# Attention and token/channel mixer on one core: the first seven slots laid out by hand, token weights loaded plainly, a last output tile sent in pieces

## The chip, the cores and the metric

The kernel runs on one core of one Trainium2 chip. A core has a matrix engine (TensorE, "PE" in the profile, its weight loads "PEld"), a vector engine (VectorE, "DVE"), an activation engine (ScalarE, "ACT"), a general engine (GpSimd, "POOL") and a queue engine (SyncE, "SP") that here only issues DMA transfers. Each runs its own list of instructions in order and waits on semaphores. The metric is the time of one execution on the device in microseconds (us), the median of several runs.

## What is computed

The reference is cosine attention followed by a mixer (batch 8, 12 heads, sequence 448, head size 64):

```python
q_n = q / (norm(q) + 1e-06);  k_n = k / (norm(k) + 1e-06)
scores = q_n @ k_n.T / tau
attn = exp(scores - max);  attn = attn / (sum(attn) + 1e-09)
x = attn @ v                                   # (8, 448, 768) once the heads are side by side
h = relu(x.T @ w_tok1) @ w_tok2                # over the sequence: 448 -> 256 -> 448
u = x + h.T
h2 = relu(u @ w_ch1) @ w_ch2                   # over the channels: 768 -> 1536 -> 768
out = u + h2
```

Since the scores are bounded, the kernel takes the exponential without subtracting the maximum.

## The kernel before, in words

Two heads make a pair, six pairs a batch, 48 pairs in all. Three pairs are a half (the index `n` of the loads), which is loaded, normed and cast together. The 448 rows of a sequence are three blocks of 128 and 64 extra rows; names with an x (`squares_x`, `scaled_x`, `score_x`) treat the extra rows.

For a pair p the steps are these. `squares` (L174 on ACT, L176 on POOL or VectorE) and `sums` (L189, L193 for the extra rows, both VectorE) give sums of squares. `rnorms` (L197 to L200) turns them into 1/(norm + 1e-6) by four activations: logarithm, exponential of half of it, logarithm of that plus 1e-6, exponential of the negative. `scaled` (L207) and `scaled_x` (L213, L218) multiply K and Q by it into the fp16 tile `kq`. `tpose` (L239, L243, L244, TensorE) transposes it into PSUM, `qk_copy` (L257, VectorE) takes it out. `score` (L297) and `score_x` (L304) multiply, and ACT takes the exponential (L298, L305). `pv` (L318, L320) multiplies with V and, on VectorE, divides by the row sum (L323, L324). `m_tok1` (L338, L341) and `m_tok2` (L357, L362, L364) are the token mixer. When a batch has its six pairs, its channel units `m_ch1` (L385, ACT L387) and `m_ch2` (L399, VectorE L402, stores L407 to L410) go into a queue, and `feed` takes units from it between the steps of later pairs. `busy` issues matmuls whose result nobody uses.

The order of the work on each engine is the order of the program text, since the schedule is manual. After a prologue for pair 0 the loop runs over slots i: a slot does the scores of pair i, `pv` of pair i−1, the token mixer of pair i−2, and norms, scaling and transposes ahead for later pairs. Tables (`sq_at`, `sum_at`, `rn_at`, `sc_at`, `cast_at`, `tok_at`, `tok2_at`) say in which slot such a step stands. `FIRST` is 6: from slot 6 on there are channel units to feed. `JOIN` is 12; up to pair 14 the transposes are TensorE's, and after that they are DMA transposes.

Loads of Q, K and V are issued on SP in order, at the start of a slot; each waits until its buffer is free. The weights are loaded on POOL's queue and cast from fp32 to fp16 in flight: `weights_tok` (L141 to L144) after the prologue, `weights_ch1` (L154) in slots 2 and 5, `weights_ch2` (L158) in slots 7 and 8. `place_w2` (L147, L150, VectorE) rearranges the second token weight at the end of slot 2. PSUM has four general buffers (tag "b", two kilobytes per partition each) that all the products share in turn, and two of double size for the scores.

The last batch's units run when nothing else is left: twelve of `m_ch1`, then `m_ch2` for the row blocks 0, 1, 2 and the block of extra rows, in two halves of 384 columns each. The block of extra rows carries 64 rows of each of two batches and is stored by two transfers (L409, L410).

## Time and profile before

| what | us |
|---|---|
| time, median of 5 runs | 401.42 (401.3 to 402.39) |
| the profiled execution, its own time | 403.68 |
| its span, first to last instruction | 401.5 |
| TensorE busy | 386.0 |
| ScalarE busy | 225.6 |
| GpSimd busy | 209.0 |
| VectorE busy | 204.8 |

The span is the stretch that the trace shows; the time of an execution is measured around it. Busy time of TensorE counts the fillers, and its matmuls overlap, so that a full TensorE is not one at its peak. In the table of stretches, the columns after the time are the busy us of each engine with the number of instructions, the granted clock of TensorE (1 is full), the share of DMA time and GB/s. A line of the timeline is start, duration, engine, line, operation, output and input tiles, and in brackets the idle time before it and who ended that. A line of the waits is the waiting engine, tile and line, then who was waited for, with the total in us, the number of times and the longest.

### The profile page before, as it was taken

How to read it: one execution, taken by the hardware profiler on the slowest of the kernel's cores; microseconds unless marked ns; L12 is line 12 of the kernel's file. 1: busy time of each engine (PE TensorE's matmuls, PEld its weight loads, DVE VectorE, ACT ScalarE, POOL GpSimd, SP SyncE). 2: the span in 40 equal slices, each digit the busy share in tenths (PEclk: the TensorE clock that was granted, in tenths of full speed). 3: DMA queues.
4: the chain of work that ended last, by engine and by line, in shares of the span. 5: the costliest groups of instructions: out<-in, count | busy, mean ns of one | idle time of the engine just before them, and what ended most of it. 6: DMA issues, size and time to landing. Idle time of an engine off the chain costs nothing.

```text
span 401.5 us, 9113 instructions
## 1 busy us (share of the span) xinstructions
PE 386.0 (96%) x3646; PEld 227.1 (57%) x3646; DVE 204.8 (51%) x463; ACT 225.6 (56%) x407; POOL 209.0 (52%) x306
## 2 busy tenths in 40 slices
PE   8789999998999999999999999999999999999995
PEld 3356465565556565566555565566555665565562
DVE  5788789465453665355544654455534353242021
ACT  5998699633666447655657436755667326601400
POOL 4987495598292949485673919486764400000000
PEclk9899999999999999999999999999999999999999
DMA  8999999999887599999996699869842733022012
GB/s 220 278 245 246 240 171 214 224 269 236 168 168 182 120 245 186 196 188 218 233 169 167 113 256 210 200 153 227 180 112 51 157 85 66 16 67 91 2 78 78
DMA packets 137194, 67.51 MB, mean 168 GB/s; under 512 B 93184, under 2 KB 133568, under 8 KB 137152
## 3 DMA queue, kind: packets, MB, share of 16 engines
q1 hardware_dynamic: 132976, 61.36, 70.4%
q0 software_dynamic: 3632, 5.18, 7.2%
q8 instruction: 28, 0.46, 0.5%
q10 hardware_dynamic: 544, 0.39, 0.3%
q14 instruction: 14, 0.11, 0.1%
HBM read 43.38 MB, written 11.01 MB: 135 GB/s over the span
## 4 chain that ended last, share of the span: by engine, by line
PE 39%; POOL 29%; issue 17%; DMA 6%; ACT 4%; DVE 3%; SPq 1%; ACTq 0%; POOLq 0%; DVEq 0%
PE psF L399 14%; PE psG L385 12%; POOL kq L207 10%; POOL sq L176 9%; DMA xv<-in_v_dram 5%; PE psO L318 3%; POOL kq L218 3%; POOL sqx L176 3%; PE psS L297 3%; ACT pt L298 2%; PE psR L338 2%; PE psU L357 2%; POOL vt L164 2%; POOL vx L168 1%; DMA km<-in_k_dram 1%
## 5 line engine op out<-in xcount | busy, mean ns | idle before, releaser
L298 ACT ACTIVATE pt<-psS 128x896 f16<-128x896 f32 x141 | 122.2, 916 | 64.6 <-PE psS L297 64.5
L385 PE MATMUL psG<-ut,wc1t 128*128 128x448 f16 x576 | 120.7, 353 | 0.0
L399 PE MATMUL psF<-wc2t,gt 128*128 128x384 f16 x672 | 116.3, 326 | 1.9 <-DVE ost L402 1.9
L387 ACT ACTIVATE gt<-psG 128x448 f16<-128x448 f32 x96 | 52.5, 547 | 74.5 <-PE psG L385 74.3
L207 POOL TENSOR_TENSOR kq<-km,rn 128x384 f16<-128x384 f32 x47 | 39.6, 843 | 94.8 <-ACT rn L200 93.5
L399 PEld LDWEIGHTS <-gt 128*128 128x128 f16 x672 | 64.2, 98 | 43.2 <-issue 3.3
L385 PEld LDWEIGHTS <-wc1t 128*128 128x128 f16 x576 | 53.2, 98 | 46.5 <-issue 4.4
L402 DVE TENSOR_TENSOR ost<-psF,ur 128x384 f32<-128x384 f32 x56 | 31.1, 556 | 76.3 <-PE psF L399 76.3
L318 PEld LDWEIGHTS <-pt 128*128 128x128 f16 x1152 | 52.7, 98 | 15.0 <-issue 3.4
L318 PE MATMUL psO<-vt,pt 128*128 128x65 f16 x1152 | 57.5, 194 | 0.0
L189 DVE TENSOR_REDUCE ssq<-sq 128x12 f32<-128x768 f32 (+1 forms) x49 | 45.2, 931 | 21.0 <-POOL sq L176 17.2
L297 PE MATMUL psS<-qk 64*128 64x448 f16 x282 | 41.1, 358 | 2.4 <-ACT pt L298 2.3
L324 DVE TENSOR_TENSOR x<-psO,rec 128x256 f16<-128x256 f32 x96 | 40.7, 424 | 3.3
L320 PE MATMUL psO<-vx,pt 128*128 128x130 f16 x192 | 41.8, 218 | 0.0
L323 DVE RECIPROCAL rec<-psO 128x4 f32<-128x4 f32 x96 | 17.1, 178 | 47.6 <-PE psO L320 47.4
L207 POOL TENSOR_TENSOR kq<-qm,rn 128x384 f16<-128x384 f32 x47 | 39.0, 829 | 0.0
L176 POOL TENSOR_TENSOR sq<-km 128x384 f32<-128x384 f32 x42 | 34.5, 823 | 2.7 <-DMA km<-in_k_dram 2.5
L338 PE MATMUL psR<-x,w1t 128*128 128x128 f16 x384 | 29.4, 219 | 0.1
L367 DVE TENSOR_TENSOR ut<-psU,xT 128x448 f16<-128x448 f32 (+2 forms) x39 | 17.6, 476 | 20.1 <-PE psU L357 20.0
L357 PE MATMUL psU<-w2t,r 128*128 128x448 f16 x96 | 25.9, 353 | 0.7 <-DVE x L324 0.4
L305 ACT ACTIVATE pt<-psX 128x448 f16<-128x448 f32 x48 | 26.5, 553 | 0.0
L176 POOL TENSOR_TENSOR sq<-qm 128x384 f32<-128x384 f32 x30 | 24.7, 823 | 0.8
(75 smaller groups left out, 324.5 us busy)
## 6 DMA issues: line engine op xcount, KB each, us to landing
vm<-in_v_dram SPq DMA_DIRECT2D x16, 576.0 KB, 5.6
out_dram<-ost SPq DMA_DIRECT2D x24, 384.0 KB, 3.8
qm<-in_q_dram SPq DMA_DIRECT2D x15, 576.0 KB, 5.2
km<-in_k_dram SPq DMA_DIRECT2D x15, 576.0 KB, 5.1
wc1t<-in_moe_w_ch_dram POOLq DMA_DIRECT2D x2, 1152.0 KB, 13.9
wc2t<-in_moe_w_ch_dram POOLq DMA_DIRECT2D x2, 1152.0 KB, 14.7
out_dram<-ost SPq DMA_DIRECT2D x8, 192.0 KB, 4.0
xq<-in_q_dram SPq DMA_DIRECT2D x7, 192.0 KB, 5.7
```

The lines of the kernel that those rows point to most:

```text
L176: eng.tensor_tensor(out=out, in0=src, in1=src, op=ALU.mult)
L189: nc.vector.tensor_reduce(out=ssqs[p // HP % 3][:, lo + 6 * a0:lo + 6 * a1], in_=sq[p][:, a0:a1].rearrange("p a g e -> p (a g) e"), axis=A ...
L207: eng.tensor_tensor(out=kqs[n % 2][:, j, a, 0:NC, :].rearrange("p c (g e) -> p g c e", g=2), in0=src, in1=_bcast_free(rn, E), op=ALU.mult)
L297: nc.tensor.matmul(psS[:, g, 0:S], qk[r, P * c:P * (c + 1)], qk[r, 512:512 + S], start=True, stop=True)
L298: nc.scalar.activation(out=pt[:, 2 * S * c:2 * S * (c + 1)].rearrange("p (g s) -> p g s", g=2), in_=psS[:, :, 0:S], func=AF.Exp, scale=inv ...
L318: nc.tensor.matmul(psO[:, mm, E1 * g:E1 * (g + 1)], pt[:, at:at + P], vt[:, 2 * j + g, c, 0:E1], start=(g == 0 and c == 0), stop=False)
L320: nc.tensor.matmul(psO[:, mm, :], pt[:, PX + lo:PX + lo + P], vx[:, j, 0:2 * E1], start=False, stop=True)
L324: nc.vector.tensor_tensor(out=xs[p][:, 2 * a:2 * a + 2, :].rearrange("p m (g e) -> p m g e", g=2), in0=o[:, :, :, 0:E], in1=_bcast_free(re ...
L338: nc.tensor.matmul(psR[:, tt, :], w1t[:, m, tt * P:(tt + 1) * P], xs[p][:, m, :], start=(m == 0), stop=(m == NC))
L385: nc.tensor.matmul(psG[:], wc1t[:, dt, ct * P:(ct + 1) * P], ut[:, dt, sp], start=(dt == 0), stop=(dt == DT - 1))
L387: nc.scalar.activation(out=gt[:, ct, sp], in_=psG[:], func=AF.Relu)
L399: nc.tensor.matmul(psF[:], gt[:, ct, lo:lo + P], wc2t[:, ct, dh * DH:(dh + 1) * DH], start=(ct == 0), stop=(ct == CT - 1))
```

## The change

It rewrites the prologue and slots 1 to 6, and the end.

- The token weights are loaded as fp32 by three plain transfers on SP, behind the first loads and ahead of those of slot 0. `place_w1` (new, slot 2) and `place_w2` (now slot 3) cast them on VectorE.
- `rnorms` is split: `norms` does the first two activations, and `inverses` adds 1e-6 and takes the reciprocal on VectorE. The prologue's pairs 1 and 2 and the extra rows, and half 1, use the two; other places keep the four activations.
- In the prologue the norms, scaling and transposes of pair 0 stand ahead of the sums of pair 1. Q of pair 0 gets a PSUM tile of its own. There are 14 fillers at the start instead of 18, and fillers are added between later steps. VectorE takes part of the scaling of pair 1 and all extra rows of half 0. The squares of pair 3 stand in the prologue.
- Slots 1 and 2 are written out. All squares of half 1 come by slot 1, all its scaling by slot 2. The extra rows of half 1 are scaled in two steps.
- Slots 3 to 6 take the token mixer in a changed order; in slot 6 ACT does the relu of pair 5 and the evictions of the second token product of pairs 4 and 5.
- The last batch computes its block of extra rows second. Its last row block is computed in pieces of 384, 256 and 128 columns, each stored on its own.

The core of the diff:

```diff
     def weights_tok():
-        nc.gpsimd.dma_start(out=w1t[:, 0:NC, :], in_=moe_w_tok1[0:SM].rearrange("(p c) t -> p c t", c=NC))
-        nc.gpsimd.dma_start(out=w1t[0:XR, NC, :], in_=moe_w_tok1[SM:S])
-        w2n.append(mix.tile([P, TT, S], FP16, name="w2n", tag="gt16", bufs=1))
-        nc.gpsimd.dma_start(out=w2n[0][:], in_=moe_w_tok2.rearrange("(tt p) s -> p tt s", p=P))
+        t = mix.tile([P, NC * T + T + TT * S], FP32, name="wtok", tag="gt16", bufs=1)
...
+        nc.sync.dma_start(out=wtok[0], in_=moe_w_tok1[0:SM].rearrange("(p c) t -> p c t", c=NC))
+        nc.sync.dma_start(out=wtok[1], in_=moe_w_tok1[SM:S])
+        nc.sync.dma_start(out=wtok[2], in_=moe_w_tok2.rearrange("(tt p) s -> p tt s", p=P))
+
+    def place_w1():
+        nc.vector.tensor_copy(out=w1t[:, 0:NC, :], in_=wtok[0])
+        nc.vector.tensor_copy(out=w1t[0:XR, NC, :], in_=wtok[1])
...
-    def rnorms(n, c0=0, c1=45):
+    def norms(n, c0=0, c1=45):
         ssq, rn = ssqs[n % 3][:, c0:c1], rns[n % 3][:, c0:c1]
         nc.scalar.activation(out=rn, in_=ssq, func=AF.Ln, bias=tiny[:])
         nc.scalar.activation(out=rn, in_=rn, func=AF.Exp, scale=0.5)
+
+    def inverses(n, c0=0, c1=45):
+        rn = rns[n % 3][:, c0:c1]
+        nc.vector.tensor_scalar_add(out=rn, in0=rn, scalar1=EPS_NORM)
+        nc.vector.reciprocal(out=rn, in_=rn)
...
-        busy(w, 18)
+        busy(w, 14)
         squares(0, nc.scalar, nc.scalar)
         sums(0, 0, 1)
         sums(0, 1, 2)
+        rnorms(0, 9, 21)
         squares(1, nc.scalar, nc.gpsimd)
-        rnorms(0, 9, 21)
+        squares_x(0, nc.scalar, nc.gpsimd)
+        scaled(0, nc.vector, nc.vector)
+        tpose_main(0, pst, 0)
+        nc.scalar.copy(out=qks[0][:, 0:SM], in_=pst[:, 0:SM])
+        tpose_main(0, psq, 1)
+        nc.vector.tensor_copy(out=qks[0][:, 512:512 + SM], in_=psq[:, 512:512 + SM])
         sums(1)
...
         sums_x(0)
...
         score_main0(0, 2)
+        norms(0, 0, 33)
+        inverses(0, 0, 33)
+        score_main0(1)
         squares(2, nc.scalar, nc.gpsimd)
...
         scaled_x(0, nc.vector, 0, 1)
...
+        scaled(1, nc.gpsimd, nc.vector)
+        scaled_x(0, nc.vector, 1, HP)
         score_rest0()
         score_x(0)
-        weights_tok()
+        busy(w, 3)
+        norm_begin(3, nc.scalar, nc.gpsimd)
+        sums(2)
+        qk_copy(1, tpose(1))
+        norms(0, 33, 45)
+        inverses(0, 33, 45)
         cast_v(0)
-        scaled(2, nc.gpsimd)
+        scaled(2, nc.gpsimd, nc.gpsimd)
...
+            elif i == 1:
+                score(1, 0, 2)
+                score(1, 1)
+                squares(4, nc.scalar, nc.gpsimd)
+                pv(0, 0)
+                sums(3)
+                score(1, 2)
+                score_x(1)
+                next_qk(2)
+                squares(5, nc.scalar, nc.gpsimd)
+                sums_x(1)
+                norms(1, 0, 21)
+                sums(4)
+                inverses(1, 0, 21)
+                sums(5)
+                scaled(3, nc.gpsimd, nc.gpsimd)
+                scaled_x(1, nc.gpsimd, 0, 1)
+                pv(0, 1)
+            elif i == 2:
+                score(2, 0, 2)
+                score(2, 1)
+                norms(1, 21, 45)
+                pv(1, 0)
+                inverses(1, 21, 45)
+                idle(4)
+                score(2, 2)
+                score_x(2)
+                next_qk(3)
+                place_w1()
+                pv(1, 1)
+                idle(2)
+                scaled(4, nc.gpsimd, nc.gpsimd)
+                scaled_x(1, nc.gpsimd, 1, HP)
+                cast_v(1)
+                scaled(5, nc.gpsimd, nc.gpsimd)
+                weights_ch1(0)
             elif 0 < i < NP_ALL and not (i > JOIN and i % 2):
-                score(i, 0, 2 if i < 4 else 0)
+                score(i, 0)
                 score(i, 1)
+                if i == 3:
+                    m_tok1(0)
+                    place_w2()
+                if i == 4:
+                    tok2(1)
+                if i < FIRST:
+                    m_tok1(i - 2)
...
             if i == FIRST:
-                next_sq([9])
-                m_tok1(i - 2)
                 pv(i - 1, 0)
+                m_tok1(i - 2)
                 pv(i - 1, 1)
-                tok2(i - 2)
-                m_tok1(i - 1)
+                scaled_x(2, nc.vector, 0, 1)
+                norm_sums(7)
+                m_tok2(i - 2, nc.scalar)
+                m_tok1(i - 1, nc.scalar)
                 next_qk(i)
-                tok2(i - 1)
+                tok2(i - 1, nc.scalar)
+                next_sq([9])
                 norm_sums(8)
...
+        last = b == B - 1
+        for m in (0, NC, 1, 2) if last else range(NC + b % 2):
+            for i0, i1 in ((0, 3), (3, 5), (5, 6)) if last and m == 2 else ((0, 3), (3, 6)):
+                units.append((ns(P * (i1 - i0), CT), lambda m=m, i0=i0, i1=i1:
+                              m_ch2(b, m, i0, i1, last and m == 2)))
```

`idle(n)` takes a PSUM tile and runs n fillers into it. In `m_ch2` the arguments i0 and i1 are the first and last block of 128 columns, and the last argument sends the piece as soon as it is evicted.

## The prediction

> **What bounds the kernel now.** I read the busy table by stretches first, because the shares of the page are means over stages with different limits.
>
> ```profile
> 10.00:14.00 4.00, 1.43 (x15) 0.67 (x16) 3.27 (x8) 3.55 (x9) 3.92 (x7) 1.00 1.14 306
> 14.00:18.00 4.00, 4.00 (x35) 1.85 (x31) 2.66 (x5) 3.94 (x12) 3.80 (x7) 0.57 1.16 246
> 18.00:22.00 4.00, 3.02 (x41) 1.73 (x40) 3.44 (x8) 3.90 (x10) 3.50 (x5) 1.00 1.18 271
> 22.00:26.00 4.00, 3.54 (x48) 2.16 (x45) 3.02 (x9) 3.61 (x9) 3.09 (x5) 1.00 1.17 245
> 30.00:34.00 4.00, 3.63 (x57) 2.54 (x55) 3.96 (x9) 3.10 (x7) 2.00 (x4) 1.00 1.09 256
> ```
>
> The columns are PE, weight loads, DVE, ACT, POOL, clock, DMA share, GB/s. From 10 to 34 us four engines are nearly full at once and TensorE waits for them; from 14 to 18 its clock is 0.57. After 60 us TensorE hardly idles: in the table of waits of that stretch it waits for anything but itself only 3.2 us, of which these two count:
>
> ```profile
> PE psF L399 <- DVE ost L402: 1.9, 2, 1.1
> POOL vt L164 <- DMA vm<-in_v_dram: 4.8, 1, 4.8
> ```
>
> They are one story: POOL's cast of the fifth V half waits for its load until 76.4, its squares end at 81.5, VectorE's sums at 82.5, and TensorE idles 0.83 before 83.1 and 1.05 before 91.6. What arrives early at 80 us can wait there. Then the end of the timeline and the head's anchors:
>
> ```profile
> 27.16 0.90 POOL L154 DMA_DIRECT2D wc1t<-in_moe_w_ch_dram  x1
> ...
> 42.40 1.30 PE L385 MATMUL psG<-ut,wc1t 128*128 128x448 f16 x6
> ...
> 396.60 0.56 DVE L402 TENSOR_TENSOR ost<-psF,ur 128x384 f32<-128x384 f32 x1 [1.39 <-PE psF L399]
> 397.19 0.50 SPq L409 DMA_DIRECT2D out_dram<-ost  x1
> 397.74 0.58 SPq L410 DMA_DIRECT2D out_dram<-ost  x1
> ```
>
> The first channel weights are issued at 27.16, land 13.9 us later by the rows of that line (41.1), and are first used at 42.40: 1.3 us of slack. The last matmul ends at 396.58, and 4.9 us of span follow.
>
> **What the skill says.** "SBUF — State Buffer", Who interferes with whom: GpSimd and a VectorE copy, cast or two-input operation share a port pair as a lock, and the later one blocks. The trace agrees: VectorE's 64x128 product at 10.69, beside POOL products, took 0.89, while a 128x384 one beside an idle POOL took 0.55. "DMA: Bandwidth & Descriptors", Queues, rings and completion order: an engine takes turns between queues packet by packet. It agrees: from 36 to 37 us POOL's queue moved 99 packets and SP's 102. "TensorE: Matmul & The Clock Gate", What's actually happening: a cold array runs at half rate and is warm after some 3.4 us of work. The halving agrees (filler matmuls 0.43 us apart until 7.3, then about half that); the warming took 5.9 us here.
>
> **The change part by part.** Durations are distances between neighbours in the timeline.
>
> *First scores.* VectorE now does sums(1) at 6.83 ahead of the scaling of pair 0 (7.71), whose norms are ready at 6.91. After: scaling at 6.93, 0.78 earlier. Fourteen fillers end at 7.35, so TensorE is free for the transposes; with its own PSUM tile the Q copy need not follow ACT's copy. Scores start near 9.15 instead of 10.08: −0.9.
>
> *The rest of pair 0.* sums(1) 0.87 and sums_x 0.66 now follow the Q copy (8.6): 10.2. norms 0.6: 10.8. The inverses on VectorE are two operations on 33 columns; the nearest row is the 4-column reciprocal, 0.18, so 0.3 together (bounds 0.2 and 0.5): 11.1. The extra-row scaling for pair 0, partly blocked by POOL's scaled(1), 1.3 (it took 1.8 before): 12.4. The transposes that wait for it started at 12.56, so the 0.9 is spent. sums(2) no longer stands before the copies (13.1 instead of 13.4), but VectorE has new work before qk_copy(1): half of scaled(1) 0.5, the extra rows of pairs 1 and 2 0.8 (bounds 0.7 and 1.5), sums(2) 0.9: copy from 15.3 to 15.9 instead of 15.45 to 16.1. Score(1) then starts near 15.95, not 16.32, on a warm array: −0.4.
>
> *Slots 1 and 2.* VectorE then has inverses 0.3, cast 0.73, pv 0.55, sums(3) 0.87, copy(2) 0.57, sums_x 0.66, sums(4) 0.87, inverses 0.3: 4.8, with 0.5 of waiting for pv's matmuls, so the inverses for pair 3 are ready at 21.3. POOL gets scaled(3) then; before, it began at 19.77. It loses the three token-weight issues (2.4 us, 12.84 to 15.2), half of scaled(1) 0.8 and 1.5 of extra rows, but 4.7 us saved are idled away, first for the K load of pairs 3 to 5 (some 13.7, from bytes queued ahead of it at the shown rates), then for those inverses. scaled(3) 1.6, its extra rows 1.1: 24.0 against 23.74. Score(3) starts near 25.4, before 25.6: −0.2.
>
> *Slot 3.* VectorE: place_w1 (768 and 256 columns from fp32; from the 1152-column cast, 0.73) 0.7, pv 0.55, cast 0.73, relu 0.34, place_w2 1.15 (as before, though it reads fp32), relu 0.34, pv 0.55, copy(4) 0.57: 4.9 from 25.1, so score(4) near 30.1, before 30.24. VectorE is the bound there.
>
> *Slots 4 to 6.* tok2(1) moves into slot 4 (0.6 more), tok2 copies and the relu of pair 5 move to ACT, which idled 4.3 us before 43.7; cover is plain. TensorE's own rows (score 0.49, tok1 0.45, tok2 0.57, pv 0.5 twice, score and extra rows 0.5, transposes 0.62) carry it to the first channel unit near 41.7: −0.7.
>
> *What is late next.* POOL's issue of the channel weights now stands behind scaled(5): from 21.3, scaled(3) 1.6, rows 1.1, scaled(4) 1.6, rows 1.5, casts 0.8, scaled(5) 1.6 = 29.5, 2.3 later. The landing is 12.3 (the shortest such row, a wc2t) to 13.9 later: 41.8 to 43.4. TensorE, there at 41.7, waits up to 1.7. I take the middle, 42.5: head zero at 42.4. The second half is issued near 33 instead of 38.1, but queues behind the first.
>
> *Token weights on SP.* Three issues of 0.6 ahead of loads(0), whose first was at 14.18; their users come at slot 3 (28 us), so hidden by 5 us or more. Packets double in bytes (0.92 MB fp32, 0.46 counted before): −0.5 to +1.9 us of a DMA that is full until 50 us and has gaps at 51 to 53 (76 GB/s in one us) and 58 to 60 (21 to 30 GB/s). I take zero, because reads are the same.
>
> *Tail.* Before: eviction 0.58, a second issue 0.55 behind the first, landing 2.70 from issue, 1.06 to the end of span: 4.9. After: eviction of 128 columns 0.29 (by the 384-column row less its columns), 0.03, landing 2.3 (a whole undisturbed tile; bounds 2.0 and 2.6), 1.06: 3.7. Twelve matmuls of 128 columns at 0.056, from the eight of psR in 0.45, cost what their columns cost. −1.2 (−0.9 to −1.5).
>
> Sum: 0 in the head, −1.2 in the tail: span 401.5 to 400.3. The profiled execution took 403.68, 2.2 more than its span; the median is 401.42. Taking −1.2 off the median gives 400.2.
>
> **The rivals.** *Head gain survives.* VectorE's order isn't the limit and the warm clock counts: at half clock the transposes took 1.08 instead of 0.62, the filler 1.0 for 0.43, the first scores 0.93 for 0.49, 1.5 in all. If that reaches the channel units, and the V load comes earlier through the gaps at 51 and 58 us, 401.42 − 1.2 − 1.5 = 398.7. For it: SP waited 2.1 for POOL's scaling before the load at 49.4, so loads follow compute. Against: VectorE's sum above.
>
> *Stall cancels tail.* The weights land at 43.5, +1.1, and it is carried: 401.3. Against: the idle 1.88 at 83 and 91 us absorbs a delay if the V load stays put.
>
> *Slower.* Same place: VectorE's fp32 casts (0.7, 0.73, 1.15 in slots 2 and 3) hold the port against POOL, the issue slips to 31.5, landing at 45.4, +3.0 at 42.4. Loads that wait for scaling slip too, so nothing absorbs it: 401.4 − 1.2 + 3.0 = 403.2. It decides from a landing at 44.4 on (2.0 less 1.2 is 0.8). Against: before, the same casts stood beside POOL work and cost it 0.3.
>
> **How the numbers follow.** 0.2%, or 0.8 us, is about what a measurement of this kernel tells from no change. Head zero: 0.45, range 399.6 to 400.8, 0.06 of it within 0.2%. Gain survives: 0.24 (397.7 to 399.4). Stall cancels: 0.19 (400.8 to 402.2). Slower: 0.12 (402.2 to 404). Faster 0.39 + 0.24 = 0.63, same 0.06 + 0.19 = 0.25, slower 0.12. The range 398.0 to 402.3 leaves out about 0.05 below and 0.11 above.
>
> **What would show it.** Scaling of pair 0 at 6.9 and scores near 9.2; transposes of the extra rows still near 12.4; scaled(3) on POOL after 21; issue of the first channel weights near 29.5 and first channel matmul at 42 to 43 with idle in front of it; last eviction about 0.3 us, span ending 3.7 after the last matmul. Wrong if POOL reaches scaled(3) before 20, if the weights are issued before 28, or if the head moves the waits at 83 and 91 instead of filling them.

## The result, and the profile after

The changed kernel takes 403.34 us (median of 44 runs, 402.46 to 405.47); the kernel before took 401.73 beside it (79 runs). The ratio is 1.0038 (95% interval 1.003 to 1.0046): slower by 0.4%, where a gain of 0.3% was forecast. The profiled execution of the changed kernel took 403.97, its span is 402.2. One thing has to be added on the profile before: that execution (403.68) lay 2.0 above its kernel's median, and the two waits at 83 and 91 us that the prediction quotes are what set it apart (see the first experiment).

The table of stretches of the changed kernel (columns: PE, weight loads, DVE, ACT, POOL, each in busy us with its instructions, then granted clock, DMA share, GB/s):

```profile
10.00:14.00 4.00, 2.81 (x19) 0.99 (x17) 2.76 (x9) 2.84 (x6) 0.93 (x1) 1.00 1.14 301
14.00:18.00 4.00, 2.73 (x24) 1.29 (x24) 3.54 (x9) 3.10 (x8) 1.99 (x5) 1.00 1.13 260
18.00:22.00 4.00, 3.44 (x37) 2.42 (x37) 2.46 (x5) 3.13 (x6) 3.48 (x4) 0.57 1.10 321
22.00:26.00 4.00, 3.56 (x41) 1.62 (x37) 3.90 (x11) 3.06 (x7) 1.93 (x4) 1.00 1.18 225
30.00:34.00 4.00, 3.61 (x58) 2.62 (x55) 3.97 (x11) 2.45 (x5) 3.80 (x6) 1.00 1.01 291
```

Before, POOL was busy 3.92 and 3.80 of the first two stretches. Now it is busy 0.93 and 1.99: it stands still for 5 of 8 us. Most of what the change took from it here (4.7 us by the prediction's count) became idle time, and its later work is still to be done. The half clock, 0.57, moved from 14:18 to 18:22. VectorE is full at 22:26, where before it had 3.02, and again at 30:34.

The timeline, in the form of the lines shown of before:

```profile
24.19 0.83 POOL L224 TENSOR_TENSOR kq<-km,rn 128x384 f16<-128x384 f32 x1 [2.08 <-DVE rn L211]
...
33.65 1.00 POOL L162 DMA_DIRECT2D wc1t<-in_moe_w_ch_dram  x1
...
46.02 0.23 PE L263 MATMUL pst<-id,kq 128*128 128x128 f16 x1 [1.01 <-DVE kq L235]
...
46.90 1.30 PE L411 MATMUL psG<-ut,wc1t 128*128 128x448 f16 x6
...
399.05 0.29 DVE L429 TENSOR_TENSOR ost<-psF,ur 128x128 f32<-128x128 f32 x1 [0.25 <-PE psF L426]
```

Of these, the scaling of pair 3 was before:

```profile
19.77 0.83 POOL L207 TENSOR_TENSOR kq<-km,rn 128x384 f16<-128x384 f32 x1 [0.50 <-ACT rn L200]
```

The scaling of pair 3 starts on POOL at 24.19 (before 19.77), the first channel weights are issued at 33.65 (27.16), the first channel matmul starts at 46.90 (42.40). The end is better: the last eviction takes 0.29 and the span ends 3.2 after the last matmul, where it took 4.9.

TensorE's waits of the first 60 us (us in total, times, longest):

```profile
PE pst L263 <- DVE kq L235: 2.0, 2, 1.0
...
PE psO L338 <- DVE vt L172: 1.2, 1, 1.2
PE pst L259 <- DVE kq L224: 1.2, 1, 1.2
```

And the chain of work that ended last, in the head (start, duration, what):

```profile
8.48 7.64 DMA xq<-in_q_dram
16.14 0.52 ACT sqx L182
16.67 0.21 ACT rn L205
...
17.14 0.38 DVE rn L210
...
17.55 0.23 DVE rn L211
17.78 0.74 DVE vt L172
...
18.56 0.49 PE psO L338 x6
...
22.84 0.86 DVE ssq L197
23.70 0.09 DVE rn L210
...
24.19 1.62 POOL kq L224 x2
```

A load of Q's extra rows, landing at 16.12, is now on the path. ACT's squares of pair 3, which the change put into the prologue, wait for it; the norms of pair 2 stand behind them on ACT, the inverses and then the cast of V behind these on VectorE, and TensorE's first product with V behind that. VectorE's sums and inverses follow, and only then can POOL scale pair 3.

### The profile page after: what moved, and what is told of

Read it like the earlier page. It is cut to its first block, busy times and chain, and to the rows that moved or that the text cites. A ratio compares the mean times of both kernels' runs of the same rounds, so it can differ in the third digit from the quotient of the medians.

```text
span 402.2 us, 9176 instructions
## 1 busy us (share of the span) xinstructions
PE 387.7 (96%) x3670; PEld 228.3 (57%) x3670; DVE 209.7 (52%) x478; ACT 223.8 (56%) x396; POOL 207.4 (52%) x304
## 4 chain that ended last, share of the span: by engine, by line
PE 67%; POOL 9%; issue 7%; DMA 5%; DVE 5%; ACT 4%; SPq 1%; ACTq 0%; POOLq 0%
PE psF L426 22%; PE psG L411 21%; PE psO L338 6%; PE psS L317 5%; PE psR L358 4%; PE psU L380 3%; POOL kq L224 3%; DMA xq<-in_q_dram 3%; POOL sq L184 3%; PE psX L324 2%; ACT pt L318 2%; PE psO L340 2%; POOL sqx L184 1%; DMA km<-in_k_dram 1%; DMA qm<-in_q_dram 1%
## 5 line engine op out<-in xcount | busy, mean ns | idle before, releaser
L426 PE MATMUL psF<-wc2t,gt 128*128 128x384 f16 (+2 forms) x684 | 116.3, 323 | 0.0
L429 DVE TENSOR_TENSOR ost<-psF,ur 128x384 f32<-128x384 f32 (+2 forms) x57 | 31.3, 549 | 78.1 <-PE psF L426 78.1
L184 POOL TENSOR_TENSOR sq<-km 128x384 f32<-128x384 f32 x43 | 35.4, 824 | 7.4 <-DMA km<-in_k_dram 3.6
L224 POOL TENSOR_TENSOR kq<-qm,rn 128x384 f16<-128x384 f32 x46 | 38.1, 829 | 0.0
```

Of the source, the lines that this page charges most:

```text
L184: eng.tensor_tensor(out=out, in0=src, in1=src, op=ALU.mult)
L224: eng.tensor_tensor(out=kqs[n % 2][:, j, a, 0:NC, :].rearrange("p c (g e) -> p g c e", g=2), in0=src, in1=_bcast_free(rn, E), op=ALU.mult)
L426: nc.tensor.matmul(psF[:, 0:w], gt[:, ct, lo:lo + P], wc2t[:, ct, P * i0:P * i1], start=(ct == 0), stop=(ct == CT - 1))
```

## The experiments

All times are medians; each ratio is to the kernel before on the same chip, with its 95% interval. The runs were spread over several chips, on which the kernel before itself took 401.55 to 402.24, so rows are best compared by their ratios. The anchors are starts in each kernel's profiled execution: score of pair 1, then the distances to score of pair 3, to score of pair 5 and to the first channel matmul (FCM). One execution can differ from the next by some 0.6 in such a distance: the run without the first weight's casts has the changed kernel's order until 27 us, but for one longer clear on POOL at 3 us, and shows 10.72 where that one shows 11.33.

| kernel | us | ratio, interval | score 1 | to 3 | to 5 | to FCM | FCM |
|---|---|---|---|---|---|---|---|
| before (profile shown above) | | | 16.32 | 9.24 | 9.11 | 7.73 | 42.40 |
| changed | 403.34 | 1.0038 (1.003 to 1.0046) | 16.82 | 11.33 | 9.99 | 8.76 | 46.90 |
| before + changed end | 399.15 | 0.9938 (0.9924 to 0.9952) | 16.41 | 9.15 | 9.12 | 7.73 | 42.41 |
| that + ACT in slot 6 | 399.75 | 0.9934 (0.9908 to 0.996) | 16.54 | 9.35 | 9.12 | 7.68 | 42.69 |
| that end + pair 0 first | 401.38 | 0.9973 (0.9963 to 0.9982) | 18.60 | 9.20 | 9.12 | 7.72 | 44.64 |
| prologue of before, changed slots and end | 401.9 | 1.0004 (0.9993 to 1.0015) | 16.34 | 9.59 | 8.66 | 9.50 | 44.09 |
| that, three parts undone | 401.5 | 0.9988 (0.9979 to 0.9998) | 16.30 | 10.33 | 9.35 | 8.24 | 44.22 |
| changed, inverses on ScalarE | 403.19 | 1.0055 (1.0032 to 1.0078) | 16.79 | 9.87 | 10.05 | 8.76 | 45.47 |
| changed, fillers before V | 404.22 | 1.0058 (1.0041 to 1.0075) | 16.86 | 11.63 | 9.99 | 9.07 | 47.55 |
| changed, token weights cast by POOL's queue | 402.03 | 1.0004 (0.9988 to 1.002) | 16.79 | 10.30 | 8.65 | 9.04 | 44.78 |
| changed, token loads later on SP | 403.24 | 1.0037 (1.0024 to 1.005) | 16.83 | 11.27 | 9.99 | 8.76 | 46.85 |
| changed, no casts of the first weight | 403.45 | 1.0042 (1.0026 to 1.0057) | 16.86 | 10.72 | 9.84 | 8.76 | 46.18 |
| changed, norms of pair 3 early | 403.83 | 1.004 (1.0028 to 1.0051) | 16.84 | 11.33 | 10.22 | 8.77 | 47.16 |
| changed, V cast first | 403.34 | 1.0043 (1.0027 to 1.0058) | 16.83 | 11.19 | 9.98 | 8.78 | 46.78 |
| changed, squares of pair 3 late | 403.68 | 1.0053 (1.0038 to 1.0067) | 16.90 | 10.82 | 9.98 | 8.76 | 46.46 |
| the last two together | 403.85 | 1.0051 (1.0039 to 1.0063) | 16.88 | 11.48 | 9.75 | 8.77 | 46.88 |
| changed, rows of pair 6 on POOL | 403.93 | 1.0056 (1.0037 to 1.0075) | 16.81 | 11.94 | 9.97 | 8.24 | 46.96 |
| that + channel weights early | 403.86 | 1.0063 (1.0045 to 1.0082) | 16.52 | 12.50 | 10.45 | 8.24 | 47.71 |
| changed, inverses, token weights, rows undone | 402.81 | 1.0011 (0.9998 to 1.0025) | 16.93 | 10.80 | 8.65 | 9.03 | 45.41 |
| changed, five parts undone | 402.87 | 1.003 (1.002 to 1.004) | 16.94 | 11.02 | 9.36 | 8.24 | 45.56 |

The changed kernel's 4.5 us at the first channel matmul are thus 0.50 + 2.09 + 0.88 + 1.03.

### The end alone

```diff
-    def m_ch2(b, m, dh):
+    def m_ch2(b, m, i0, i1, send=False):
...
+        for m in (0, NC, 1, 2) if last else range(NC + b % 2):
+            for i0, i1 in ((0, 3), (3, 5), (5, 6)) if last and m == 2 else ((0, 3), (3, 6)):
```

> The kernel before with the changed end alone (block of extra rows second, last row block in pieces of 384, 256 and 128 columns). Theory (the head loses, the tail gains): the same last matmul as before, 396.6, and 1.7 us less after it, so 0.4% faster than before (ratio 0.996). Rival (the end is hidden behind the fixed cost of a store): ratio 1.000.

399.15: 2.4 below the kernel before (401.55), and below both kernels of this case. Its timeline ends with:

```profile
394.46 0.29 DVE L403 TENSOR_TENSOR ost<-psF,ur 128x128 f32<-128x128 f32 x1 [0.25 <-PE psF L400]
```

Its span ends at 397.3, 2.9 after the last matmul: 2.0 less than before. The head is the same (first channel matmul at 42.41), and the waits at 83 and 91 us are gone, though nothing there was changed. So those waits belonged to that one execution. From the first channel matmul to the start of the last eviction, 352.05 us pass in this run's profile, and 352.05 to 352.67 in those of all kernels of the table with the changed end but one (353.22, see below); in the profile before it was 354.20. The time outside the span is 1.85, and the other 0.3 to 0.4 of the gain lies there: before, the profiled execution's is 2.2. What follows: the end is worth about 2.4, and a delay that the head has at its first channel matmul is carried to the end: there is no idle for it to vanish in.

### Pair 0 first, alone

Before with the changed end, and the prologue's start in the changed order; the other parts as before.

```diff
+        squares_x(0, nc.scalar, nc.gpsimd)
         scaled(0, nc.vector)
         tpose_main(0, pst, 0)
+        nc.scalar.copy(out=qks[0][:, 0:SM], in_=pst[:, 0:SM])
...
+        sums(1)
+        sums_x(0)
         busy(w, 2)
         score_main0(0, 2)
+        rnorms(0, 0, 33)
         scaled(1, nc.gpsimd)
```

> The kernel before with the changed end, and with the start of the prologue as the change has it: pair 0 normed, scaled and transposed ahead of the sums of pair 1, Q in its own PSUM tile, 14 fillers; norms of the extra rows and pair 1 in one call of four activations after the first scores. All else as before. Theory (the 0.9 us at the first scores is given back, since the extra rows of pair 0 wait for sums that now come later): first scores at 9.3 instead of 10.1, transposes of the extra rows of pair 0 at 12.6 or later, first channel matmul not before 42.4, time equal to or up to 2 us above the kernel with the changed end alone (399.2). Rival (the reordering pays): first channel matmul at 41.6, 398.4.

401.38, and the first channel matmul is 2.23 later than in the run of the end alone. In the profile this is carried in full (352.37 to the last eviction, against 352.05). The medians of the two runs differ by 2.23 too, but they are from two chips; by the ratios, 0.9973 against 0.9938, the loss is 1.4, with some 0.7 of uncertainty to either side. The delay arises before the score of pair 1. TensorE's wait and VectorE's timeline in this kernel:

```profile
PE pst L243 <- DVE kq L218: 2.7, 1, 2.7
```

```profile
12.13 0.28 DVE L213 TENSOR_TENSOR kq<-xq,rn 64x128 f16<-64x128 f32 x1 [1.27 <-ACT rn L200]
12.34 1.64 DVE L218 TENSOR_TENSOR kq<-xk,rn 64x64 f16<-64x64 f32 x2
```

The extra rows of pair 0 are scaled at 12.13, since their norms now come behind the sums of pair 1 and the first exponentials; and two products of 64x64 take 1.64 beside POOL's scaling of pair 1, which starts at the same time. The 0.3 gained at the first scores pays little of the 2.7 us that TensorE then waits for these products.

### The changed slots with the prologue of before, and with three parts undone

```diff
-        busy(w, 14)
+        busy(w, 18)
         squares(0, nc.scalar, nc.scalar)
         sums(0, 0, 1)
         sums(0, 1, 2)
+        squares(1, nc.scalar, nc.gpsimd)
         rnorms(0, 9, 21)
-        squares(1, nc.scalar, nc.gpsimd)
...
+        weights_tok()
         cast_v(0)
         scaled(2, nc.gpsimd, nc.gpsimd)
+        norm_begin(3, nc.scalar, nc.gpsimd)
+        qk_copy(1, tpose(1))
```

> The prologue of before (token weights cast on POOL's queue, no cast on VectorE), with slots 1 to 6 and the end of the changed kernel. Theory (the prologue's new order costs some 2.2 us, which the run with that order alone showed, and the token-weight casts most of the rest): score(1) near 16.4, score(2) near 20.3, first channel matmul at 42.3 to 43.3, time 399 to 400. Rival (the rearrangement of slots 1 to 6 is itself what costs, whatever the prologue): first channel matmul at 44.5 or later, time 401 or more.

401.9, with the first channel matmul at 44.09: between the end alone and the changed kernel, and the rival's time. Score of pair 1 and the way to pair 3 are nearly as before (16.34, 9.59 against 9.15 to 9.24). So 1.74 of the changed kernel's 2.09 in slots 1 and 2, with its 0.50 at score 1, come from what its prologue and its token weights leave behind: 2.24 in all. The run before this one lost about as much with the reorder alone, but there ahead of pair 1 and here mostly after it; that the two are one loss is not shown. Slots 3 and 4 are faster than before (8.66 against 9.11): the changed order of these slots gains 0.45. Slots 5 and 6 lose it:

```profile
42.47 0.23 PE L257 MATMUL pst<-id,kq 128*128 128x128 f16 x1 [1.01 <-DVE kq L229]
...
44.09 2.42 PE L405 MATMUL psG<-ut,wc1t 128*128 128x448 f16 x6 [0.58 <-DMA wc1t<-in_moe_w_ch_dram]
```

TensorE waits 1.01 for the rows of pair 6 on VectorE, then 0.58 for the weights, and the first six channel matmuls take 2.42, not 1.30; the clock of 42:46 is 0.77. So the first channel matmul flatters this run: 353.22 us pass from it to the last eviction, 1.17 more than in the run of the end alone. In time the old prologue and the old loading of the token weights bring back 1.0038 − 1.0004, or 1.4 us, of a head that costs 1.0038 − 0.9938, or 4.0; the rest is lost by the changed slots even behind the old prologue.

The second run takes three suspects away:

```diff
-                norms(1, 0, 21)
-                inverses(1, 0, 21)
+                rnorms(1, 0, 21)
...
-                scaled_x(2, nc.vector, 0, 1)
...
+                weights_ch1(0)
                 scaled(4, nc.gpsimd, nc.gpsimd)
...
                     scaled(6, nc.gpsimd, nc.gpsimd)
+                    scaled_x(2, nc.gpsimd, 0, 1)
```

> The run with the prologue of before and the changed slots 1 to 6, with three things more: inverses on ScalarE, extra rows of pair 6 on POOL at the end of slot 5, first channel weights issued ahead of the scaling of pair 4. Theory (in that run slots 5 and 6 lost 2.9 us to the weights' landing and to the wait for those rows, slots 1 and 2 lost 0.35 to the inverses, slots 3 and 4 gained 0.46): score of pair 6 at 43.3 to 44.2 instead of 46.44, time 398.8 to 399.9, level with before plus the changed end (399.15). Rival (slots 5 and 6 lose for another reason, the norms of pair 6 being later): score of pair 6 at 45 or later, time 400.5 or more.

401.5, score of pair 6 at 45.45: the rival's side. The last stretch falls to 8.24, still 0.5 above before. It waits 0.50 for POOL's rows of pair 6, since POOL idles 5.26 for the norms of pair 6, which the change moved from slot 4 to the end of slot 5. And slots 1 and 2 rise to 10.33: with four activations the norms hold the scaling of pair 3 by 1.99, where the inverses on VectorE held it 1.53.

### Inverses back on ScalarE, in the changed kernel

```diff
-        norms(0, 0, 33)
-        inverses(0, 0, 33)
+        rnorms(0, 0, 33)
```

and likewise at the three other places.

> The changed kernel with the four inverses back on ScalarE, as two more activations behind the norms. Theory (VectorE's list is what the head waits for): each inverse took 0.4 to 0.6 us of VectorE, the first channel matmul comes 1 to 2 us before 46.9, total 0.5 to 1.5 us less than the changed kernel. Rival (clock): the gap before the first pv stays, no change beyond 0.3 us. Rival (DMA): no change.

403.19, within the spread of the changed kernel. Its profiled execution is 1.4 ahead at the first channel matmul, but it ran at full clock throughout, which the changed kernel's did not. Among executions at full clock (a mean of 0.999 or 1.000) the medians are 402.96 (5) and, for the changed kernel, 403.0 (24). The inverses cost more on VectorE than forecast, and where they run decides nothing that the times show.

### The token weights

On POOL's queue with the cast in flight, as before, and no casts of the first weight on VectorE:

```diff
-        nc.sync.dma_start(out=wtok[0], in_=moe_w_tok1[0:SM].rearrange("(p c) t -> p c t", c=NC))
+        nc.gpsimd.dma_start(out=w1t[:, 0:NC, :], in_=moe_w_tok1[0:SM].rearrange("(p c) t -> p c t", c=NC))
...
-                place_w1()
```

> The changed kernel with the token weights again cast in flight by POOL's queue, issued in the prologue while POOL waits; no casts of the first weight on VectorE. Theory (VectorE's list): 1.6 us of casts and their lock on POOL go, score of pair 4 starts 1 to 1.8 us earlier than 33.75, total 0.5 to 1.5 us less than the changed kernel. Rival (clock): nothing before slot 3 changes, total the same. Rival (DMA order): the load of the extra rows that ScalarE waits for at 16.1 and later loads land as before, same total.

402.03, 1.3 below the changed kernel, and with a ratio of 1.0004 level with the run that had the whole prologue of before as well. Slots 3 and 4 take 8.65 instead of 9.99, and slots 1 and 2 10.30 instead of 11.33. The chain that ends last now runs through the channel weights:

```profile
32.03 12.71 DMA wc1t<-in_moe_w_ch_dram
```

Then the plain loads issued behind those of slot 0, casts kept:

```diff
             if i < DMA_FROM:
                 loads(i)
+            if i == 0:
+                weights_tok()
```

> The changed kernel with the three plain loads of the token weights issued on SP behind the loads of slot 0 instead of ahead of them (issue some 9 us later, near 24; the casts stay). Theory (the order of the loads is hidden, what costs is the casts and the work around them): first channel matmul within 0.5 of the changed kernel's 46.90, time within 0.5 of 403.3. Rival (the loads ahead of slot 0's cost): first channel matmul at 45.9 or earlier, time 402.3 or less. The casts may now wait for their load, which would make it slower by what that wait shows.

403.24, first channel matmul at 46.85: no difference. Their place ahead of the loads of slot 0 is hidden, as the prediction had it. That they are on SP at all, and not on POOL's queue, is not tested by this. Last, the casts of the first weight left out. In this kernel the weight is zero, cleared by POOL at the start, so the token mixer adds nothing and only the timing is of use:

```diff
-                place_w1()
```

> The changed kernel without the two casts of the first token weight in slot 2 (the weight is zero instead, cleared by POOL at the start, so the token mixer adds nothing); the plain loads stay. Theory (the casts on VectorE cost, not the loads on SP ahead of slot 0's): score(3) near 26.6 instead of 28.15, first channel matmul near 45.2, time 1.0 to 1.5 below the changed kernel's, as with the weights cast on POOL's queue (402.03 against 403.34). Rival (the transfers on SP ahead of the loads of slot 0 cost): score(2) stays at 22.6, score(3) near 27.6 or later, first channel matmul at 46.4 or later, time within 0.5 of the changed kernel's.

403.45: no gain in the time. The view by stretches and the timeline of this kernel show that its profile is disturbed; the third line is the same group of matmuls in the run with the prologue of before:

```profile
26.00:30.00 4.00, 4.00 (x37) 2.40 (x37) 2.36 (x6) 1.82 (x3) 3.81 (x7) 0.60 1.17 234
```

```profile
28.44 1.89 PE L358 MATMUL psR<-x,w1t 128*128 128x128 f16 x16
```

```profile
26.42 1.07 PE L352 MATMUL psR<-x,w1t 128*128 128x128 f16 x16
```

The array ran at half clock in slot 3: 0.8 more for this group, 0.4 more for the scores next to it (0.93, not 0.55). Without these 1.2, slots 3 and 4 would take some 8.6 (an estimate), as with POOL's queue. The times, however, do not show the casts to be the 1.3:

| median us (executions) | mean clock 0.999 or 1.000 | 0.995 or 0.996 |
|---|---|---|
| changed | 403.0 (24) | 403.7 (16) |
| no casts of the first weight | 402.6 (2) | 403.9 (4) |
| token weights cast by POOL's queue | 401.5 (8) | 402.8 (5) |

At like clock, leaving the casts out gained 0.5 at most, and the other move 0.9 to 1.5. Some 0.3 of that lies at the very end: from the start of the last eviction to the end of the span it is 3.1 to 3.2 in all eleven kernels that load the token weights on SP, and 2.8 to 2.9 in the eight with the changed end that load them on POOL's queue. Why, and what the rest of the gain is, stays open.

### The clock

```diff
                 squares(4, nc.scalar, nc.gpsimd)
+                idle(6)
                 pv(0, 0)
```

> The changed kernel with six fillers between the first two scores of slot 1 and pv of pair 0, where TensorE idles 1.2 us. Rival (clock): TensorE stays at full clock from 18 to 22 us, score of pair 2 starts 1.3 us earlier, and most of it is kept at the first channel matmul (45.6 instead of 46.9). Theory (VectorE's list): the clock is full, but what follows waits for VectorE and POOL, so the first channel matmul moves less than 0.5 us.

404.22. The clock of 18:22 was 1.00 and the score of pair 2 still started at 22.70 (changed: 22.63): what it waits for doesn't come earlier. The half clock is not what the head lost; the changed kernel's own executions at full clock still take 403.0.

### The links of the chain

VectorE's list in slot 1 in another order, then the two links that the chain shows, one at a time and together.

```diff
+                sums_x(1)
+                norms(1, 0, 21)
+                inverses(1, 0, 21)
                 squares(4, nc.scalar, nc.gpsimd)
```

> The changed kernel with the sums, norms and inverses for pair 3 ahead of the squares of pair 4 and the last scores of pair 1. Theory (the order on VectorE in slot 1 makes POOL's scaling of pair 3 late, 24.2 instead of 19.8): that scaling starts near 21.5, score of pair 3 at 26 to 27 instead of 28.15, the weights of the channel mixer are issued 2 us earlier, and 1 to 2 us of it arrive at the first channel matmul. Rival (VectorE is simply full): the time lost by what is pushed back equals what is won, first channel matmul within 0.5 us of 46.9.

```diff
+        cast_v(0)
         norms(0, 33, 45)
         inverses(0, 33, 45)
-        cast_v(0)
```

> The changed kernel with the cast of the first V half on VectorE ahead of the norms and inverses of pair 2 instead of behind them. Theory (the chain that ends last runs through the load of the extra rows of Q, which lands at 16.12, ACT's squares of pair 3, the norms and inverses of pair 2, this cast and the first product with V at 18.56): that product near 17.5, the array waits less than 0.3 there, score(2) near 21.6, first channel matmul some 1.0 earlier, time 402.3 to 402.8. Rival (VectorE's whole list up to the inverses of pair 3 sets scaled(3), the cast only changes places): scaled(3) on POOL still at 24 or later, first channel matmul at 46.6 or later, time within 0.4 of 403.3.

```diff
-        norm_begin(3, nc.scalar, nc.gpsimd)
         sums(2)
...
         scaled(2, nc.gpsimd, nc.gpsimd)
+        norm_begin(3, nc.scalar, nc.gpsimd)
```

> The changed kernel with the squares of pair 3 behind the scaling of pair 2 in the prologue instead of ahead of the norms of pair 2. Theory (ACT's squares wait for the load of the extra rows of Q until 16.14, and the norms of pair 2 behind them): those norms at 16.15 to 16.2 instead of 16.57 (the sums of pair 2 end at 16.12), product with V 0.4 earlier, first channel matmul 0.3 to 0.5 earlier, time 402.8 to 403.1. Rival (the squares of pair 3 are themselves what is next on the path): sums of pair 3 later by 1 us or more, first channel matmul no earlier than 46.9, time 403.3 or more.

> Both of the two preceding edits. Theory: the product with V near 17.5, first channel matmul 1.0 to 1.5 earlier than 46.90, time 402.0 to 402.5. Rival (VectorE's list or POOL's list is full whatever the order): within 0.4 of 403.3.

403.83, 403.34, 403.68 and 403.85: none gains. Each edit does what it should at its place. With the norms of pair 3 early, POOL scales pair 3 at 23.36, but its score still starts at 28.17 (28.15 in the changed kernel). With the cast first, the first product with V starts at 17.82 instead of 18.56, with the squares late at 18.00, with both at 17.54 and without any wait. Then the next thing is late. In the run with the squares late (VectorE, then POOL):

```profile
17.25 0.70 DVE L172 CAST vt<-vm 128x1152 f16<-128x1152 f32 x1
...
20.23 0.96 DVE L197 TENSOR_REDUCE ssq<-sq 128x12 f32<-128x768 f32 x1 [0.90 <-POOL sq L184]
...
23.75 0.83 POOL L224 TENSOR_TENSOR kq<-km,rn 128x384 f16<-128x384 f32 x1 [1.53 <-DVE rn L211]
```

The cast is 0.5 earlier, and the sums of pair 3 now wait for POOL's squares. In the changed kernel and in the three with the cast first, the squares late, or both, the scaling of pair 3 starts between 23.75 and 24.19. The load wait is real, but it is one of several of about the same length.

### Slots 5 and 6

```diff
-                scaled_x(2, nc.vector, 0, 1)
...
                     scaled(6, nc.gpsimd, nc.gpsimd)
+                    scaled_x(2, nc.gpsimd, 0, 1)
```

> The changed kernel with the extra rows of pair 6 scaled on POOL at the end of slot 5 instead of on VectorE in slot 6. Theory (TensorE's wait of 1.01 us for that product at 46.02 is carried): first channel matmul at 45.9, just behind the landing of its weights at 45.65, time 0.8 to 1.0 below the changed kernel's. Rival (POOL's product comes no earlier than VectorE's, or the weights land later than that): first channel matmul at 46.6 or later, time the same.

```diff
+                weights_ch1(0)
                 scaled(4, nc.gpsimd, nc.gpsimd)
...
-                weights_ch1(0)
```

> As the run with the extra rows of pair 6 on POOL, and the first channel weights issued one step earlier, ahead of the scaling of pair 4 instead of behind that of pair 5: issue near 28 instead of 33.65, landing near 41. Theory (the landing was only the next limit, close behind): first channel matmul at 45.5 to 45.9, time within 0.3 of that run. Rival (the landing is what holds TensorE from slot 6 on): first channel matmul at 45 or earlier and time lower by 0.5 or more.

Both reach the first channel matmul 8.24 after the score of pair 5, not 8.76: the wait of 1.01 for VectorE becomes one for POOL:

```profile
46.08 0.23 PE L263 MATMUL pst<-id,kq 128*128 128x128 f16 x1 [0.49 <-POOL kq L235]
```

Issuing the weights at 27.59 adds nothing, so in the changed kernel their landing at 45.65 was not what TensorE waited for. The times (403.93 and 403.86) are not lower: in the profiled executions slots 1 and 2 took 11.94 and 12.50, against 11.33, which loses more than the half us gained. Nor does the half us last. In the run with the rows on POOL, TensorE waits twice for POOL's scaling of the next pair:

```profile
52.29 0.34 PE L259 MATMUL pst<-id,kq 128*128 128x128 f16 x3 [0.58 <-POOL kq L224]
53.08 0.34 PE L259 MATMUL pst<-id,kq 128*128 128x128 f16 x3 [0.45 <-POOL kq L224]
```

The changed kernel has one such wait, of 0.45. From the first channel matmul to the last eviction it takes 352.15, these two runs 352.67 and 352.66, so that the 0.52 is given back.

### Together, and ACT in slot 6

Inverses on ScalarE, token weights on POOL's queue and rows of pair 6 on POOL at once:

> The changed kernel with three parts undone together: inverses on ScalarE, token weights cast by POOL's queue, all extra rows of half 2 scaled on POOL. Theory (three separate loads on VectorE and on its port shared with POOL): the gains add, 2.1 and 1.4 us at the first channel matmul from the first two and 0.5 from the third, so it comes near 43 instead of 46.9 and the time near 400.5. Rival (one hidden limit, such as a load or POOL's own list): less than 3 us together, 401.5 or more.

402.81, no better than the token weights alone. And five edits at once (V cast first, squares of pair 3 late, token weights on POOL's queue, rows of pair 6 on POOL, channel weights early):

> Both of these edits, the token weights cast on POOL's queue without casts on VectorE, the extra rows of pair 6 on POOL, and the first channel weights issued ahead of the scaling of pair 4. Theory (the parts found so far make up most of the loss): product with V near 17.5, score(3) near 26.0, first channel matmul at 43.0 to 44.0, time 399.6 to 400.8. Rival (each part only uncovers the next limit): first channel matmul at 44.8 or later, time 401.3 or more. Either way it stays behind the kernel before with the changed end alone (399.15).

402.87, first channel matmul at 45.56: the rival's side. The gains don't add. With a ratio of 1.003 against 1.0004 the five are even slower than the token weights alone. POOL's line for the scaling of pair 3 in this run:

```profile
24.00 0.83 POOL L218 TENSOR_TENSOR kq<-km,rn 128x384 f16<-128x384 f32 x1 [1.52 <-DVE rn L205]
```

It is still 4 us later than before. The last piece, on the run of the end alone: the relu of pair 5 and the two evictions of slot 6 on ACT.

```diff
-                tok2(i - 2)
-                m_tok1(i - 1)
+                tok2(i - 2, nc.scalar)
+                m_tok1(i - 1, nc.scalar)
                 next_qk(i)
-                tok2(i - 1)
+                tok2(i - 1, nc.scalar)
```

> The kernel before with the changed end and one part of slot 6: ScalarE takes the relu of pair 5 and the evictions of the second token product of pairs 4 and 5. Theory (VectorE's list around slot 6 counts): ScalarE idled 4.3 us there, first channel matmul 0.2 to 0.5 us before 42.4, 0 to 0.5 us less than the changed end alone. Rival (TensorE's own work is the limit there): equal to the changed end alone, 399.2.

399.75, first channel matmul at 42.69: neither gain nor loss beyond the spread.

## Why the prediction was wrong

**The first scores: right.** Scaling of pair 0 came at 6.79 (forecast 6.93), scores at 9.32 (9.15). Right, too, was the remark that this is spent at once: the transposes of the extra rows came at 13.08, later than before (12.56) and than forecast (12.4). The 0.4 that was then to be won at the score of pair 1 was not: forecast 15.95, it started at 16.82, after 16.32 before.

**Slots 1 and 2: the step that failed.** The prediction had VectorE's inverses for pair 3 ready at 21.3; they were ready at 24.1. Its list of operations was complete, its sum of waits was not. VectorE's timeline:

```profile
11.09 0.18 DVE L210 TENSOR_SCALAR rn<-rn 128x33 f32<-128x33 f32 x1 [0.65 <-ACT rn L206]
11.31 0.36 DVE L211 RECIPROCAL rn<-rn 128x33 f32<-128x33 f32 x1
...
17.14 0.37 DVE L210 TENSOR_SCALAR rn<-rn 128x12 f32<-128x12 f32 x1 [0.38 <-ACT rn L206]
17.55 0.23 DVE L211 RECIPROCAL rn<-rn 128x12 f32<-128x12 f32 x1
...
19.64 0.18 DVE L343 RECIPROCAL rec<-psO 128x4 f32<-128x4 f32 x1 [1.13 <-PE psO L340]
```

Against the forecast: the copy of pair 1 ended at 16.77, 0.87 later than the forecast 15.9; 0.38 of wait for norms that stood on ACT behind a wait for a load; inverses 0.55 and 0.50 where 0.3 twice was put, 0.45; 1.13 of wait for the products with V and 0.38 for the transposes of pair 2 where 0.5 was put, 1.0. These are 2.7 of the 2.8. The prediction said itself that POOL would idle, "first for the K load", and then for these inverses, but it counted on the removed POOL work to make up for that idling by 24.0. POOL was busy 2.9 of the stretch from 10 to 18 where it had been busy 7.7, and the scaling of pair 3 slipped from 19.77 to 24.19. No single link mended it. In the profiled executions that scaling came back to 22.69 with the inverses on ScalarE, to 23.12 with the token weights on POOL's queue and to 21.97 with the whole prologue of before; the times show a gain for the last two alone, 1.4 each, of the 4.0.

**Slot 3: a size.** The casts of the first token weight were put at 0.7 and took 1.63 (27.80 to 29.43). Behind the prologue of before, and without these casts, the order of these slots gained 0.45; in the changed kernel's profile slots 3 and 4 lost 0.88, where the forecast had VectorE's list as long as before. (In the few executions of the run without the casts, the times give them 0.5 at most.) The Trainium skill's page "SBUF — State Buffer", Who interferes with whom, which the prediction drew on, has VectorE and GpSimd share a port pair as an exclusive lock; this fits, though no run here sets it apart from other causes. In the profile of the changed kernel, two products of 64x64 on VectorE beside POOL's scaling of pair 1 took 1.10, and two of 64x128, at 14.64 beside an idle POOL, 0.58. The cast of 128x768 took 1.08 at 27.80 beside POOL's scaling; another of that size, in another layout, took 0.67 at 31.11, while two casts on POOL took 1.71 that had taken 0.75 at 17.15.

**What is late next: wrong place.** The landing of the channel weights was forecast for 41.8 to 43.4 and came at 45.65, since the issue followed POOL's list to 33.65 (forecast 29.5). But TensorE arrived later still. The issue 6 us earlier changed nothing; the extra rows of pair 6, to which the prediction gave no price, held TensorE for 1.01.

**Absorption: not there.** The rival in which a stall cancels the tail's gain rested its objection on 1.88 of idle at 83 and 91 us. It was a feature of the profiled execution, not of the kernel: the run of the end alone has neither, and in every other profiled kernel the delay at the first channel matmul is there at the last eviction too. The sign to be seen was in the figures before: 403.68 for that execution, 401.42 for the median. The prediction set both side by side and did not ask where the difference lay.

**The tail: undersized.** Forecast −1.2. The eviction took 0.29 as forecast; the last store, 64 KB, landed 1.5 after its issue, not 2.3; and the time beyond the span shrank. Together −2.4.

So the sum 0 − 1.2 should have read +4.0 to +4.5 − 2.4. At the median it was +1.6, which puts the head at 4.0; the anchor of 4.5 is that of a profiled execution 0.6 above the median. The rival "Slower" named a time (403.2) close to the measured one, and a landing (45.4) close to 45.65, by luck: of its mechanism, casts that hold the port until the weights are late, the times show 0.5 at most, and the weights' landing is none of it.

What stays open is how the 4.0 divides. The load wait, the place of the inverses and the order of VectorE's list were each undone alone and showed no gain in time. The token weights back on POOL's queue gained 1.4 by the ratios, but the whole prologue of before with them gained no more, and the changed slots lose in other places when they are reached earlier. The sharing of pair 1's scaling with VectorE and the added fillers were never undone by themselves.

## What to carry to other kernels

Where four engines are nearly full in turn, as here, moving one pair's chain ahead can push the others' back; count what each engine's list has to do before the operation that the next stage waits for, waits included, and treat idle time on any of them as a loss until something is shown to repay it. An execution that is profiled above its kernel's median may hold waits that the median doesn't have; nothing should be booked against them. Change the end and the head in separate steps: here the end alone gives 399.15, a ratio of 0.9938, and the head gives it all back and 1.6 us more.

## What the runs showed of the hardware

- The stretch of half clock lay at different places in kernels of nearly the same order. It fell into 14 to 18 us before, 18 to 22 in the changed kernel's profile, 26 to 30 in the run without the first casts, and was absent in the run with the squares late. Executions of the changed kernel whose mean clock was 0.999 or 1.000 (24 of 44) have a median of 403.0, those at 0.995 or 0.996 (16) 403.7. So a spread of some 0.7 goes with it; also without it the changed kernel is behind.
- Two operations on 12 to 33 columns of 128 rows (add, reciprocal) took 0.5 to 0.6 together on VectorE in the changed kernel, the four activations of `rnorms` 1.1 on ScalarE.
- A store of 64 KB landed 1.5 us after its issue, of 128 KB 1.7, of 384 KB 2.3 (profile of the changed kernel).
